# Building the attention mask by slots, queries and keys in one transfer, two weight transfers from ScalarE's queue

## The chip, the cores and the metric

The kernel runs on one core of a Trainium2 chip. Its time is device microseconds (us) of one execution; shown is the median of three runs. One further execution was recorded by the hardware profiler, and every duration below comes from it. PE is TensorE, DVE VectorE, ACT ScalarE, POOL GpSimd, SP SyncE, which issues nearly all transfers.

## The reference

An attention with a band and a few global keys is followed by two feed-forward layers, all in float32:

```
scores = (q @ k^T) / sqrt(64)            # 2 batches, 8 heads, 768 tokens, 64 per head
rel    = query position - key position
keep   = (key < n_global) | (0 <= rel < n_local)          # 8 and 96 at run time
dist   = n_local where only the global rule keeps a key, else |rel|
scores = where(keep, scores - slope[head] * dist, -1e9)
x      = softmax(scores) @ v                              # 1536 tokens x 512
h      = x @ w_in;   x = softplus(h) @ w_out              # 512 -> 2048 -> 512
h      = x @ w_in2;  y = (h * clip(h + 3, 0, 6) / 6) @ w_out2
```

The weights arrive as 64-bit numbers. `n_global` and `n_local` are inputs too, so the mask is computed on the chip.

## The kernel before

**Attention.** The 1536 tokens are 12 blocks of 128 queries. A block needs its own keys, the block before (the band is 96 wide) and the global keys, which are laid over the first 32 columns of the block before. Work goes in quads: `att_s(k)` takes four heads of one block, two quads to a block. A quad has eight score matmuls in the trace for a block with neighbours (`s`, L516; each of the four float32 matmuls runs as two), then four rows on DVE (`pm`, L522: scores plus bias, and the row minimum of the negated sum), four exponentials on ACT (L527), the reciprocal of the sums on DVE (`rs`, L409 and L410), four multiplications by it on POOL (L412), transposes on PE (`ptp`, L550), a copy out of PSUM on ACT (`pT`, L552), and the product with the values on PE (`px`, L568). In the text q0, q1, q2 are the first quads: q0 and q1 belong to block 0, which has no block before and so 128 columns a row; from q2 on a row has 256.

**The mask.** `bias` holds, for each of the 8 heads, three slabs of 128x128: slab 0 for a block's own keys, slab 1 for the block before, slab 2 for a first block (own keys and global keys in one). They are made from `far`, a distance in which forbidden places are huge. L461 to L476 make `far` for all three slabs at once; `counts()` (L780) turns the two integers, which are 64-bit in memory, into floats first. Then ACT multiplies slab 2 by each head's slope (L478, eight operations), and DVE does slabs 0 and 1 in one operation for each head (`bias_of`, L482: four heads ahead of q0, four after it).

**Transfers.** All are issued on SP's queue, in program order: `ns` (the counts), then for each block `qT` and `kT` (queries and keys, laid out by head; block 0 in two pieces each, L442 and L443) and `V` (L447), then the weights (L114). A weight unit is 512 KB.

**Weights.** `unit_convert` (L117 to L146) splits one unit into a high and a low part: absolute value on ACT (L133), clamp on POOL (L136), three integer operations on DVE (L137, L140, L141), a rounding copy on ACT (L145), a subtraction on DVE (L146). The first feed-forward layer needs the high and low parts of the first two units before its first matmul (`hf`, L193).

**Order.** L654 to L661 run the lead: three quads of scores ahead, then for each of five steps some filling matmuls on zeros (`warm`, L651; `FILL`), the transposes, and `LEAD_UNITS` weight units. Before all that stand `WARM` = 12 such matmuls. PE's instructions keep the order in which they are written (`ordered`). The other engines' order comes from a scheduler, except where `keep_in_program_order` fixes it. Each engine works through its own list strictly in turn. After the lead, `Layers.run` weaves the remaining quads into the first layer's matmuls.

**The check.** `check_step` (L615) verifies near the end that the inputs fit the fast way, and sets a flag by which a general way would be taken.

## Time and profile before

| what | value |
|---|---|
| median of 3 runs | 635.11 us (634.53 to 635.13) |
| the profiled execution | 633.73 us |
| its span, first to last instruction | 631.9 us |
| PE busy | 613.0 us, 97% of the span |
| DVE busy | 426.0 us, 67% |
| ACT busy | 381.0 us, 60% |
| POOL busy | 137.3 us, 22% |
| mean granted PE clock | 0.996 |

A busy PE is not PE at its peak: the ends of matmuls are modelled and overlapping ones are merged. The shares are means over stages that differ: while attention and weight conversion run, DVE and ACT are full, and later PE alone is. What a change in the first microseconds is worth is read from that stretch, and from what carries it to the end. 1.8 us of the profiled time lie outside the span.

### The profile page before, as it was taken

What the parts mean: (1) busy time and instruction counts of PE and PEld (TensorE: products, weight loads), DVE (VectorE), ACT (ScalarE), POOL (GpSimd) and SP (SyncE); (2) the same over time, 40 slices, a digit from 0 to 9 for tenths busy, and PEclk for the clock granted to TensorE, in tenths of its full rate; (3) what the DMA queues carried; (4) which work ended last, traced back from release to release, by engine and by line L of the source; (5) the groups of instructions that cost most, each with busy time, mean ns of one, the idle gap of its engine ahead of it and who ended that gap; (6) DMA issues with size and microseconds to landing.
All of it is one profiled execution on the core that took longest, in us unless ns stands there. A gap on an engine that the chain in (4) does not pass through costs nothing.

```text
span 631.9 us, 9656 instructions
## 1 busy us (share of the span) xinstructions
PE 613.0 (97%) x3496; PEld 513.8 (81%) x3496; DVE 426.0 (67%) x893; ACT 381.0 (60%) x808; POOL 137.3 (22%) x180
## 2 busy tenths in 40 slices
PE   8779999999999999999999999999999999999997
PEld 4568987899999888877788888888888888888886
DVE  6988587735799999999998996224943423424252
ACT  6977888774777877777687852425786222222130
POOL 3665454531122233523200410000100000000000
PEclk9989999999999999999999999999999999999999
DMA  8744131011234243333311142001372000001011
GB/s 271 251 170 155 55 101 56 23 26 67 67 106 163 74 158 107 129 103 124 112 62 39 62 134 100 1 1 34 102 248 85 0 1 0 2 0 67 1 67 69
DMA packets 25076, 53.62 MB, mean 85 GB/s; under 512 B 2496, under 2 KB 9152, under 8 KB 25024
## 3 DMA queue, kind: packets, MB, share of 16 engines
q1 hardware_dynamic: 25024, 52.96, 25.4%
q8 instruction: 28, 0.46, 0.3%
q14 instruction: 24, 0.20, 0.1%
HBM read 49.81 MB, written 3.15 MB: 84 GB/s over the span
## 4 chain that ended last, share of the span: by engine, by line
PE 71%; DVE 18%; ACT 6%; issue 2%; DMA 1%; POOL 1%; SPq 0%; POOLq 0%; ACTq 0%; DVEq 0%
PE acc L193 25%; PE h L193 24%; PE accf L193 7%; PE hf L193 6%; ACT pm L527 3%; DVE wa L140 2%; DVE wa L141 2%; PE accz L193 2%; PE hz L193 2%; PE ptp L550 2%; DVE w L146 2%; PE px L568 2%; PE s L516 1%; DVE t L179 1%; DVE t L178 1%
## 5 line engine op out<-in xcount | busy, mean ns | idle before, releaser
L193 PE MATMUL h<-xsh,w 128*128 128x512 f32 x584 | 155.8, 390 | 1.2 <-DVE t L179 1.2
L193 PEld LDWEIGHTS h<-xsh,w 128*128 128x128 f32 x584 | 109.1, 188 | 25.1 <-DVE t L179 2.7
L136 POOL TENSOR_SCALAR wa<-wa 128x512 f32<-128x512 f32 x56 | 69.1, 1239 | 241.3 <-ACT wa L133 241.2
L193 PE MATMUL acc<-w,gh 128*128 128x512 f32 x344 | 106.0, 390 | 0.0
L183 DVE SCALAR_TENSOR_TENSOR t<-t,h 128x512 f32<-128x512 f32 x43 | 29.5, 687 | 77.4 <-ACT t L182 77.3
L185 DVE TENSOR_TENSOR gl<-t,gh 128x512 fp32r<-128x512 f32 x73 | 52.3, 716 | 42.0 <-ACT gh L184 41.8
L193 PE MATMUL h<-xsl,w 128*128 128x512 f32 x292 | 80.6, 390 | 0.0
L182 ACT ACTIVATE t<-h,three 128x512 f32<-128x512 f32 x43 | 29.5, 687 | 83.4 <-PE h L193 83.2
L193 PE MATMUL acc<-gh,w 128*128 128x512 f32 x240 | 77.8, 391 | 0.9 <-ACT gh L184 0.6
L193 PEld LDWEIGHTS acc<-w,gh 128*128 128x128 f32 x344 | 64.6, 188 | 13.3
L184 ACT CAST gh<-t 128x512 fp32r<-128x512 f32 x73 | 45.3, 620 | 43.7 <-PE acc L193 20.4
L412 POOL TENSOR_SCALAR pm<-pm,rs 128x256 f32<-128x256 f32 (+1 forms) x96 | 54.2, 582 | 59.9 <-DVE rs L410 31.8
L193 PE MATMUL acc<-w,gl 128*128 128x512 f32 x172 | 67.1, 390 | 0.0
L193 PEld LDWEIGHTS h<-xsl,w 128*128 128x128 f32 x292 | 54.8, 188 | 11.4
L193 PE MATMUL accf<-ghf,w 128*128 128x256 f32 x288 | 57.3, 288 | 0.0
L193 PEld LDWEIGHTS acc<-gh,w 128*128 128x128 f32 x240 | 44.9, 188 | 11.3 <-ACT gh L184 1.5
L527 ACT ACTIVATE pm<-pm,nm 128x256 f32<-128x256 f32 (+1 forms) x96 | 46.2, 484 | 3.3 <-DVE nm L522 3.1
L193 PE MATMUL hf<-xsh,w 128*128 128x256 f32 x288 | 47.1, 290 | 0.0
L193 PEld LDWEIGHTS accf<-ghf,w 128*128 128x128 f32 x288 | 46.6, 192 | 0.3
L193 PE MATMUL acc<-gl,w 128*128 128x512 f32 x120 | 46.8, 390 | 0.0
L146 DVE TENSOR_TENSOR w<-wa,w 128x512 fp32r<-128x512 f32 x56 | 40.3, 721 | 8.4 <-ACT w L145 8.4
L133 ACT ACTIVATE wa<-raw 128x512 f32<-128x512 f32 x53 | 35.5, 674 | 12.9 <-DVE w L146 7.0
(115 smaller groups left out, 1046.6 us busy)
## 6 DMA issues: line engine op xcount, KB each, us to landing
raw<-in_w2i SPq DMA_DIRECT2D x16, 512.0 KB, 3.3
raw<-in_w2o SPq DMA_DIRECT2D x16, 512.0 KB, 3.2
raw<-in_w1i SPq DMA_DIRECT2D x14, 512.0 KB, 3.4
raw<-in_w1o SPq DMA_DIRECT2D x12, 512.0 KB, 3.3
V<-in_v SPq DMA_DIRECT2D x12, 256.0 KB, 3.5
chk<-in_q SPq DMA_DIRECT2D x12, 256.0 KB, 2.9
chk<-in_k SPq DMA_DIRECT2D x12, 256.0 KB, 2.8
qT<-in_qt SPq DMA_DIRECT2D x11, 256.0 KB, 3.9
```

What stands on the lines that cost most here:

```text
L133: first = nc.scalar.activation(a, raw.bitcast(F32)[:, :, 1], AF.Abs)
L136: nc.gpsimd.tensor_scalar(out=a, in0=a, scalar1=W_HI, scalar2=W_LO, op0=ALU.min, op1=ALU.max)
L140: nc.vector.scalar_tensor_tensor(out=ai, in0=hi, scalar=-2 ** 30, in1=ai, op0=ALU.bitwise_and, op1=ALU.bitwise_or)
L141: nc.vector.scalar_tensor_tensor(out=ai, in0=lo, scalar=29, in1=ai, op0=ALU.logical_shift_right, op1=ALU.bitwise_or)
L146: nc.vector.tensor_tensor(out=wl, in0=a, in1=r32(wh), op=ALU.subtract)
L182: nc.scalar.activation(t1, hf, AF.Relu, bias=self.three[:, 0:1])
L183: nc.vector.scalar_tensor_tensor(out=t3, in0=t1, scalar=6.0, in1=hf, op0=ALU.min, op1=ALU.mult)
L184: nc.scalar.copy(gh, t3)
L185: nc.vector.tensor_tensor(out=gl, in0=t3, in1=r32(gh), op=ALU.subtract)
L193: return self.nc.tensor.matmul(out, lhsT=a, rhs=b, start=start and z == 0, stop=stop and z == len(seq) - 1, **kw)
L412: nc.gpsimd.tensor_scalar(out=t, in0=t, scalar1=rs[:, j:j + 1], scalar2=0.0, op0=ALU.mult, op1=ALU.add)
L527: nc.scalar.activation(pmz, pmz, AF.Exp, bias=nm[:, z:z + 1], scale=-1.0, accum_out=sm[:, z:z + 1])
```

## The change

- The mask is made by slots. `counts()` takes only the low 32-bit word of each integer (`cv`); the full conversion (`full_counts`) moves to `check_step`, which also checks that the low word was enough. `masks(0)` makes `far` for slab 0 and, from it, for slab 2; `masks(1)` makes slab 1 later, ahead of q2's rows.
- Slab 2 of the eight heads is made on three engines: heads 0 and 1 on ACT, 2 to 5 on POOL, 6 and 7 on DVE between q0's second and third row. Slabs 0 and 1 stay on DVE: heads 0 to 3 behind `masks(1)`, heads 4 to 7 behind q2's rows.
- The order on DVE is fixed by hand for this stretch: q0's and q1's reciprocals are held back (`held`) and issued behind q1's rows and behind `masks(1)` with its four slabs.
- Queries and keys of a block stand together in memory and in one buffer (`qk`, three slots); a block is one transfer of 512 KB, block 0 two of 256 KB split by heads.
- The first two weight units are issued on ScalarE's queue, behind its table load.
- The copy of the global keys (`gk`, L500) moves from ACT to POOL. `WARM` goes from 12 to 8.

Line numbers in the pieces of order below are those of the kernel they belong to. On VectorE, from the arrival of the counts to the first rows (`pm`) of q0, the list before reads (`nf`, `cneg`, `cv` are the counts, `gc`, `gfar`, `far`, `rel` the mask's pieces):

```order
L781 CAST cv<-nsb 128x4
L467 COPY rel<-rel 128x128
L782 TENSOR_SCALAR cneg<-cv 128x2
L783 TENSOR_TENSOR cneg<-cneg,cv 128x2
L784 SCALAR_TENSOR_TENSOR nf<-cneg,cv 128x2
L473 TENSOR_SCALAR gfar<-gc,nf 128x384
L474 TENSOR_SCALAR far<-rel,nf 128x384
L475 TENSOR_TENSOR far<-far,rel 128x384
L476 SCALAR_TENSOR_TENSOR far<-gfar,nf,far 128x384
L482 TENSOR_SCALAR bias<-far 128x256 x4
L522 ISA pm_193,nm_194<-s_0_191,bias 128x128
```

and in the change:

```order
L811 CAST cv<-nsb 128x4
L485 TENSOR_SCALAR late<-gc,cv 128x128
L474 TENSOR_SCALAR far<-rel,cv 128x128
L478 TENSOR_TENSOR far<-far,rel 128x128
L481 SCALAR_TENSOR_TENSOR far<-late,cv,far 128x128
L540 ISA pm_171,nm_172<-s_0_169,bias 128x128
L540 ISA nm_172 128x1
L540 ISA pm_171,nm_172<-s_1_170,bias 128x128
```

Between the counts and the first row stand four operations of 128 columns where eight small and wide ones and four slabs stood.

On VectorE between the last row of q1 and the first of q2, before (`rs_212` is q0's reciprocal):

```order
L522 ISA pm_221,nm_222<-s_1_220,bias 128x128
L522 ISA nm_222 128x1
L409 TENSOR_SCALAR rs_212<-sm_195 128x4
L522 ISA pm_250,nm_251<-s_0_248,bias 128x256
```

and in the change (`rs_188` is q0's, `rs_206` q1's):

```order
L411 TENSOR_SCALAR rs_188<-sm_173 128x4
L412 RECIPROCAL rs_188<-rs_188 128x4
L474 TENSOR_SCALAR far<-rel,cv 128x128
L478 TENSOR_TENSOR far<-far,rel 128x128
L481 SCALAR_TENSOR_TENSOR far<-late,cv,far 128x32
L498 TENSOR_SCALAR bias<-far 128x256 x4
L411 TENSOR_SCALAR rs_206<-sm_193 128x4
L540 ISA pm_231,nm_232<-s_0_229,bias 128x256
```

What stood ahead of q0 (slab 1's mask and four double slabs) now stands between q1 and q2, behind a reciprocal that waits for q0's exponentials and ahead of one step that waits for q1's.

On ScalarE from its table load to the copies of q0's transposes, before and then in the change:

```order
L770 ACT_TABLE_LOAD
L500 COPY gk<-kT 128x128
L478 ACTIVATE bias<-far 128x128 x8
L527 ACTIVATE pm_193,sm_195<-pm_193,nm_194 128x128 x4
L527 ACTIVATE pm_221,sm_223<-pm_221,nm_222 128x128 x4
```

```order
L800 ACT_TABLE_LOAD
L116 DMA part_91<-in_w1i 128x1024 x2
L489 ACTIVATE bias<-far 128x128 x2
L549 ACTIVATE pm_171,sm_173<-pm_171,nm_172 128x128 x4
L549 ACTIVATE pm_191,sm_193<-pm_191,nm_192 128x128 x4
```

Six slabs and the copy of the global keys leave ScalarE's list, and two transfers enter it.

The diff, cut:

```diff
-WARM, FILL = 12, (6, 4, 2, 0, 0)
+WARM, FILL = 8, (6, 4, 2, 0, 0)
...
+        self.n_early = 0
...
-        self.nc.sync.dma_start(out=raw.rearrange("p c t -> p (c t)"), in_=self.weights[2 * layer + u][f])
+        queue = self.nc.scalar if x < self.n_early else self.nc.sync
+        queue.dma_start(out=raw.rearrange("p c t -> p (c t)"), in_=self.weights[2 * layer + u][f])
...
-def softmax_rows(nc, sm, rs, pm):
-    nc.vector.tensor_scalar(out=rs, in0=sm, scalar1=EPS, scalar2=None, op0=ALU.add)
+def softmax_rows(nc, sm, rs, pm, keep=lambda i: i):
+    keep(nc.vector.tensor_scalar(out=rs, in0=sm, scalar1=EPS, scalar2=None, op0=ALU.add))
     nc.vector.reciprocal(out=rs, in_=rs)
     for j, t in enumerate(pm):
         nc.gpsimd.tensor_scalar(out=t, in0=t, scalar1=rs[:, j:j + 1], scalar2=0.0, op0=ALU.mult, op1=ALU.add)
...
+        layers.n_early = 2
-        ap2 = actx.enter_context(tc.tile_pool(name="ap2", bufs=3))
...
-        kT = ap1.tile([P, KC, 3, P], F32, name="kT")
+        qk = ap1.tile([P, 3, KC, 2, P], F32, name="qk")
-        qT, V, px = {}, {}, {}
+        V, px = {}, {}
...
         def load_block(n):
-            qT[n] = ap2.tile([P, KC, P], F32, tag="qT", name=f"qT{n}")
-            for cs in (slice(0, 1), slice(1, KC)) if n == 0 else (slice(0, KC),):
-                nc.sync.dma_start(out=qT[n][:, cs], in_=qt[n][:, cs])
-                nc.sync.dma_start(out=kT[:, cs, n % 3, :], in_=kt[n][:, cs])
+            for cs in (slice(0, KC // 2), slice(KC // 2, KC)) if n == 0 else (slice(0, KC),):
+                nc.sync.dma_start(out=qk[:, n % 3, cs], in_=qkt[n][:, cs])
...
         load_block(0)
+        while layers.loaded < layers.n_early:
+            layers.unit_load(layers.loaded)
+            layers.loaded += 1
...
+        rel = tp.tile([P, 2, P], F32, tag="t", name="rel")
+        gc = tp.tile([P, P], F32, tag="t", name="gc")
         far = tp.tile([P, 3, P], F32, tag="t", name="far")
-        gfar = tp.tile([P, 3, P], F32, tag="t", name="gfar")
+        late = tp.tile([P, P], F32, tag="t", name="late")
         bias = ap1.tile([P, H, 3, P], BF16, name="bias")
         iota = dict(allow_small_or_imprecise_dtypes=True)
-        nc.gpsimd.iota(rel[:, 2, :], pattern=[[-1, P]], base=0, channel_multiplier=1, **iota)
-        nc.gpsimd.iota(gc[:, 2, :], pattern=[[1, P]], base=0, channel_multiplier=0, **iota)
+        nc.gpsimd.iota(rel[:, 0, :], pattern=[[-1, P]], base=0, channel_multiplier=1, **iota)
+        nc.gpsimd.iota(gc, pattern=[[1, P]], base=0, channel_multiplier=0, **iota)
         nc.gpsimd.iota(rel[:, 1, :], pattern=[[-1, P]], base=P, channel_multiplier=1, **iota)
-        nc.vector.memset(gc[:, 0:2, :], BIG)
-        nc.vector.tensor_scalar(out=far[:, 2, :], in0=rel[:, 2, :], scalar1=0.0, scalar2=BIG, op0=ALU.is_lt, op1=ALU.mult)
-        nc.vector.tensor_tensor(out=rel[:, 2, :], in0=rel[:, 2, :], in1=far[:, 2, :], op=ALU.add)
-        nc.vector.tensor_copy(rel[:, 0, :], rel[:, 2, :])
+        nc.vector.tensor_scalar(out=late, in0=rel[:, 0, :], scalar1=0.0, scalar2=BIG, op0=ALU.is_lt, op1=ALU.mult)
+        nc.vector.tensor_tensor(out=rel[:, 0, :], in0=rel[:, 0, :], in1=late, op=ALU.add)
         nc.vector.memset(rel[:, 1, 0:MAX_GLOBAL], BIG)
-        nc.vector.tensor_copy(gc[:, 1, 0:MAX_GLOBAL], gc[:, 2, 0:MAX_GLOBAL])
-        counts()
-        ng, nl = nf[:, 0:1], nf[:, 1:2]
-
-        nc.vector.tensor_scalar(out=gfar, in0=gc, scalar1=ng, scalar2=BIG, op0=ALU.is_ge, op1=ALU.mult)
-        nc.vector.tensor_scalar(out=far, in0=rel, scalar1=nl, scalar2=BIG, op0=ALU.is_ge, op1=ALU.mult)
-        nc.vector.tensor_tensor(out=far, in0=far, in1=rel, op=ALU.add)
-        nc.vector.scalar_tensor_tensor(out=far, in0=gfar, scalar=nl, in1=far, op0=ALU.add, op1=ALU.min)
+        ng, nl = counts()
+
+        def masks(z):
+
+            tc.keep_in_program_order(nc.vector.tensor_scalar(
+                out=far[:, z, :], in0=rel[:, z, :], scalar1=nl, scalar2=BIG, op0=ALU.is_ge, op1=ALU.mult
+            ))
+            tc.keep_in_program_order(
+                nc.vector.tensor_tensor(out=far[:, z, :], in0=far[:, z, :], in1=rel[:, z, :], op=ALU.add)
+            )
+            to, n = (far[:, 2, :], P) if z == 0 else (far[:, 1, 0:MAX_GLOBAL], MAX_GLOBAL)
+            tc.keep_in_program_order(nc.vector.scalar_tensor_tensor(
+                out=to, in0=late[:, 0:n], scalar=nl, in1=far[:, z, 0:n], op0=ALU.add, op1=ALU.min
+            ))
+
+        nc.vector.tensor_scalar(out=late, in0=gc, scalar1=ng, scalar2=BIG, op0=ALU.is_ge, op1=ALU.mult)
+        masks(0)
         for h in range(H):
-            nc.scalar.mul(bias[:, h, 2, :], far[:, 2, :], -SLOPES[h] / SCALE)
-
-        def bias_of(hs):
+            if h < 2:
+                nc.scalar.mul(bias[:, h, 2, :], far[:, 2, :], -SLOPES[h] / SCALE)
+            elif h < 6:
+                nc.gpsimd.tensor_scalar(
+                    out=bias[:, h, 2, :], in0=far[:, 2, :], scalar1=-SLOPES[h] / SCALE, scalar2=0.0,
+                    op0=ALU.mult, op1=ALU.add,
+                )
+
+        def bias_of(hs, zs=slice(0, 2)):
             for h in hs:
                 tc.keep_in_program_order(nc.vector.tensor_scalar(
-                    out=bias[:, h, 0:2, :], in0=far[:, 0:2, :], scalar1=-SLOPES[h] / SCALE, scalar2=None, op0=ALU.mult
+                    out=bias[:, h, zs, :], in0=far[:, zs, :], scalar1=-SLOPES[h] / SCALE, scalar2=None, op0=ALU.mult
                 ))
 
-        bias_of(range(H // 2))
-
-        pms, pTs = {}, {}
+        pms, pTs, held = {}, {}, []
         s_tags = [(ps_s, f"s{j}") for j in range(2)]
...
                 if i == 0:
-                    nc.scalar.copy(gk, kT[:, :, slot, 0:MAX_GLOBAL])
+                    nc.gpsimd.tensor_copy(gk, qk[:, slot, :, 1, 0:MAX_GLOBAL])
+            if k == KC // 2:
+                masks(1)
+                bias_of(range(H // 2))
+                softmax_rows(*held.pop(), keep=tc.keep_in_program_order)
...
-                        ps[j][:, a, 0:nsl, :], lhsT=qT[n][hp, 2 * e + a, :], rhs=kT[hp, 2 * e + a, ks, :],
+                        ps[j][:, a, 0:nsl, :], lhsT=qk[hp, slot, 2 * e + a, 0, :], rhs=qk[hp, ks, 2 * e + a, 1, :],
...
-                nc.vector.tensor_tensor_reduce(
+                row = nc.vector.tensor_tensor_reduce(
...
+                if k < KC // 2:
+                    tc.keep_in_program_order(row)
+                if k == 0 and z == 1:
+                    bias_of(range(6, H), slice(2, 3))
                 nc.scalar.activation(pmz, pmz, AF.Exp, bias=nm[:, z:z + 1], scale=-1.0, accum_out=sm[:, z:z + 1])
-            if k == 0:
+            if k == KC // 2:
                 bias_of(range(H // 2, H))
             rs = ap_m.tile([P, 4], F32, tag="rs", name=f"rs{k}")
-            softmax_rows(nc, sm, rs, [pm[:, z, 0:w] for z in range(4)])
+            rows = (nc, sm, rs, [pm[:, z, 0:w] for z in range(4)])
+            if k == 1:
+                softmax_rows(*held.pop(), keep=tc.keep_in_program_order)
+            if k < KC // 2:
+                held.append(rows)
+            else:
+                softmax_rows(*rows)
             if e == KC // 2 - 1 and 1 <= i < NB - 1:
-                nc.scalar.copy(kT[:, :, slot, 0:MAX_GLOBAL], gk)
+                nc.scalar.copy(qk[:, slot, :, 1, 0:MAX_GLOBAL], gk)
...
-            c4 = fp.tile([1, 4], F32, name="c4")
+            c4 = fp.tile([1, 5], F32, name="c4")
+            full_counts()
             nc.vector.tensor_reduce(out=c4[:, 0:1], in_=pf, axis=AX.X, op=ALU.max)
             for z, (src, lim, op) in enumerate((
                 (c4[:, 0:1], SQ_LIMIT, ALU.is_le), (nf[0:1, 0:1], float(MAX_GLOBAL), ALU.is_le),
                 (nf[0:1, 1:2], float(MAX_LOCAL), ALU.is_le), (nf[0:1, 1:2], 1.0, ALU.is_ge),
+                (nf[0:1, 0:1], cv[0:1, 0, 0:1], ALU.is_equal),
...
         def counts():
             tc.keep_in_program_order(nc.vector.tensor_copy(cv, nsb))
-            nc.vector.tensor_scalar(out=cneg, in0=cv[:, :, 0], scalar1=0.0, scalar2=None, op0=ALU.is_lt)
+            return cv[:, 0, 0:1], cv[:, 1, 0:1]
+
+        def full_counts():
+            tc.keep_in_program_order(nc.vector.tensor_scalar(out=cneg, in0=cv[:, :, 0], scalar1=0.0, scalar2=None, op0=ALU.is_lt))
             nc.vector.tensor_tensor(out=cneg, in0=cneg, in1=cv[:, :, 1], op=ALU.add)
             nc.vector.scalar_tensor_tensor(
                 out=nf, in0=cneg, scalar=float(2 ** 32), in1=cv[:, :, 0], op0=ALU.mult, op1=ALU.add
...
-        "qt": blocks(q), "kt": blocks(k),
+        "qkt": np.ascontiguousarray(np.stack([blocks(q), blocks(k)], axis=3)),
```

## Rows read from the trace of the kernel before

**Rows 1.** Busy time by stretch: us, each engine (count), PE clock, DMA share, GB/s.

```profile
20.00:30.00 10.00, 7.09 (x68) 5.08 (x65) 9.97 (x32) 10.00 (x31) 5.84 (x8) 1.00 0.66 202
30.00:40.00 10.00, 7.48 (x74) 6.41 (x74) 10.00 (x30) 7.22 (x20) 7.82 (x12) 1.00 0.63 213
...
43.90:47.20 3.30, 3.30 (x24) 2.32 (x21) 2.23 (x10) 3.27 (x11) 1.76 (x4) 0.50 0.19 57
```

**Rows 2.** Timeline of the head: start, us, engine, line, what [idle before].

```profile
1.29 0.42 SPq L442 DMA_DIRECT2D qT<-in_qt  x1
...
1.31 5.20 PE L651 MATMUL warm<-zeros 128*128 128x512 bf16 x12 [1.31 <-DVE zeros L437]
...
3.46 0.17 DVE L781 CAST cv<-nsb 128x4 f32<-128x4 int32 x1 [1.33 <-DMA nsb<-in_ns]
...
6.29 0.30 ACT L500 COPY gk<-kT 128x128 f32<-128x128 f32 x1 [4.19 <-DMA kT<-in_kt]
...
6.44 1.16 PE L516 MATMUL s<-kT,qT 64*128 64x128 f32 x16
6.49 1.70 ACT L478 ACTIVATE bias<-far 128x128 bf16<-128x128 f32 x8
...
7.30 0.29 DVE L522 CUSTOM_DVE_ANT_0 pm<-s,bias 128x128 f32<-128x128 f32 x1
...
8.10 0.39 ACT L527 ACTIVATE pm<-pm,nm 128x128 f32<-128x128 f32 x1
```

**Rows 3.** Groups by line and form, first 34 us: count, busy us, mean ns.

```profile
L412 POOL TENSOR_SCALAR pm<-pm,rs 128x128 f32<-128x128 f32 x8 | 2.8, 373 | 9.0 <-ACT pm L527 9.0
...
L482 DVE TENSOR_SCALAR bias<-far 128x256 bf16<-128x256 f32 x8 | 1.8, 289 | 0.0
...
L410 DVE RECIPROCAL rs<-rs 128x4 f32<-128x4 f32 x6 | 1.0, 173 | 0.1
...
L466 DVE TENSOR_TENSOR rel<-rel,far 128x128 f32<-128x128 f32 x1 | 0.3, 316 | 0.0
```

**Rows 4.** Block 0's third and fourth piece: queue, size, us from issue to landing.

```profile
qT<-in_qt SPq DMA_DIRECT2D x1, 192.0 KB, 2.5
kT<-in_kt SPq DMA_DIRECT2D x1, 192.0 KB, 3.5
```

**Rows 5.** Timeline from q2's scores to the first weight unit on VectorE.

```profile
8.43 1.23 PE L516 MATMUL s<-kT,qT 64*128 64x256 f32 x8 [0.83 <-DMA kT<-in_kt]
...
9.58 1.47 PE L651 MATMUL warm<-zeros 128*128 128x512 bf16 x6
...
11.18 0.49 ACT L527 ACTIVATE pm<-pm,nm 128x256 f32<-128x256 f32 x1
...
12.68 1.13 PE L516 MATMUL s<-kT,qT 64*128 64x256 f32 x8
...
13.82 1.85 POOL L412 TENSOR_SCALAR pm<-pm,rs 128x256 f32<-128x256 f32 x4
...
15.63 0.62 POOL L136 TENSOR_SCALAR part<-part 128x512 f32<-128x512 f32 x1
...
16.84 0.40 DVE L137 TENSOR_SCALAR part<-part 128x512 int32<-128x512 int32 x1
```

**Rows 6.** Timeline, PE and VectorE, around PE's two long pauses in attention.

```profile
32.02 1.09 PE L568 MATMUL px<-pT,V 128*64 128x128 f32 x16 [3.26 <-ACT kT L533]
...
38.70 0.41 DVE L522 CUSTOM_DVE_ANT_0 pm<-s,bias 128x256 f32<-128x256 f32 x1
...
42.50 0.63 PE L550 MATMUL ptp<-ident,pm 128*128 128x128 f32 x4 [2.38 <-ACT pT L552]
```

**Rows 7.** Timeline where the check's first reduction stands, VectorE and PE's weight loads.

```profile
485.40 0.18 DVE L632 TENSOR_REDUCE m<-sq 128x1 f32<-128x24 f32 x1 [2.12 <-ACT chk L628]
...
485.91 0.69 DVE L185 TENSOR_TENSOR gl<-t,gh 128x512 fp32r<-128x512 f32 x1 [0.33 <-ACT gh L184]
...
486.65 0.19 PEld L193 LDWEIGHTS acc<-w,gl 128*128 128x128 f32 x1 [0.28 <-DVE gl L185]
```

More of the change, by code (lines that the diff above doesn't have):

```diff
@@ L412, in softmax_rows, with fast_path @@
         nc.gpsimd.tensor_scalar(out=t, in0=t, scalar1=rs[:, j:j + 1], scalar2=0.0, op0=ALU.mult, op1=ALU.add)
-def fast_path(tc, ident, three, nf, counts, q, k, qt, kt, v, weights, out, flag):
+def fast_path(tc, ident, three, nf, cv, counts, full_counts, q, k, qkt, v, weights, out, flag):
     with ExitStack() as ctx, ExitStack() as actx:
@@ L764, in general_path, with body @@
         layers.run()
-def body(tc, q, k, v, qt, kt, ns, w1i, w1o, w2i, w2o, out):
+def body(tc, q, k, v, qkt, ns, w1i, w1o, w2i, w2o, out):
     nc = tc.nc
@@ L792, in body @@
         weights = (w1i, w1o, w2i, w2o)
-        fast_path(tc, ident, three, nf, counts, q, k, qt, kt, v, weights, out, flag)
+        fast_path(tc, ident, three, nf, cv, counts, full_counts, q, k, qkt, v, weights, out, flag)
         redo = nc.values_load(flag[0:1, 0:1], min_val=0, max_val=1)
@@ L806, in blocks @@
     def blocks(a):
-        return np.ascontiguousarray(
-            a.reshape(B, KC, 2, NB, P, D).transpose(0, 3, 2, 5, 1, 4)
-        ).reshape(B * NB, P, KC, P)
+        return a.reshape(B, KC, 2, NB, P, D).transpose(0, 3, 2, 5, 1, 4).reshape(B * NB, P, KC, P)
     def words(a, axes=None):
```

2 lines of the change are left out of this document (removed).

## The prediction

> **What bounds the kernel now.** I read the page's table of engines first, then busy time by stretch, then the timeline of the first 17 us. PE is busy for 613.0 of 631.9 us, so time can come only from PE's pauses and its slow stretches. From 20 to 40 us VectorE is full, ScalarE is full for the first half, and PE has about 5.4 us of pauses [rows 1]: the end of this stretch is set by VectorE's list of rows and weight conversions. Behind it PE alone is the bound, and the order of every engine there is the same in both kernels, but for the check near the end. So the change is worth what it moves the full stretch forward, plus what it does to PE's clock in it, less what the check costs.
>
> The reader is to see three things in the timeline of the head. The first row of q0 starts at 7.30, though its scores began at 6.44: VectorE was still at four slabs. The first exponential starts at 8.10, since ScalarE had the copy of the global keys (waiting for block 0's last piece until 6.29) and eight slabs first [rows 2]. And VectorE is full only from 16.84, where the first weight unit reaches it behind POOL's work on q2 (13.82) and the clamp (15.63) [rows 5]. I call that point S.
>
> **The change, step by step** (times in the profiled span; 633.73 us is that execution, 1.38 below the median of 635.11, and differences are carried over to the median unchanged).
>
> *PE's start.* Twelve warm-ups took 5.20 us, 0.433 each; eight take 3.47, so q0's scores can start at 1.31 + 3.47 = 4.78 [rows 2]. Their data, 256 KB issued at 1.29, land 2.5 to 3.5 us later by the two pieces of 192 KB [rows 4], between 3.8 and 4.8: not later than PE. The six warm-ups at 9.58 took 1.47, 0.245 each [rows 5], so the first twelve ran at the lower level (1.2 GHz) and the later ones at 2.4. At the lower level q0's half of the 16 score matmuls takes 1.16 instead of 0.58 [rows 2]; the first row needs three quarters of it, so it starts at 4.78 + 0.87 = 5.7, against 7.30.
>
> *The mask* is no later: the counts at 3.46, 0.17 for the cast, four operations of 128 columns at no more than 0.32 each [rows 3], 0.21 for ScalarE's first slab (eight in 1.70): 5.1. POOL's four slabs are not shown before; its multiplication of the same size takes 0.37 [rows 3], so they end at 4.9 + 1.5 = 6.4, when q1 has not begun its rows. Bounds: 0.21 each (ScalarE's) to 0.46 (four of twice the size took 1.85 [rows 5]); even at 0.46 they end at 6.8, and the last of them is q1's second row's, not needed before.
>
> *ScalarE.* It loses six slabs (6 x 0.21 = 1.3) and the copy (0.3). The first exponential can follow its row by the row's 0.29 and its read-out, 0.4 as an estimate: 6.1. From 8.10 to 11.18 eight exponentials took 3.08 [rows 2, 5], so q0 and q1 end at 9.2. The two issues on its queue fall into its idle time ahead of 6.29; cost nothing.
>
> *VectorE between q1 and q2.* Eight rows and two slabs, at the 0.225 that one of four slabs adds where they overlap (0.29 alone): 5.7 + 2.2 = 7.9. Then q0's two reciprocal steps (0.17 each), slab 1's mask (two operations at 0.32 and one of 32 columns, 0.8 together), four slabs (eight took 1.8 [rows 3]), q1's first step: 7.9 + 0.35 + 0.8 + 0.9 + 0.1 = 10.0, when q1's exponentials are through. So q2's rows start at about 10.0, its exponentials at 10.4 against 11.18. This holds while block 1 lands before 9.1, since three quarters of q2's scores (0.92 of 1.23) must precede; before it landed at 8.43 [rows 5]. I take it to land as before: 192 KB of queries took 2.5 and of keys, which then went into strided pieces, 3.5 [rows 4], and now both go in long lines; but 1 MB of weights runs beside it.
>
> *The point S.* q2's exponentials end 1.96 later (4 x 0.49), at 12.4; reciprocal 0.35, POOL's four 1.85 (now nothing of q1 is in its way), clamp 0.62: S = 15.2 against 16.84, 1.6 earlier. In the change's list q3's two reciprocal steps stand behind S, before they stood ahead of it: 0.35 more to do, leaving 1.3. From S the lists hold the same rows, conversions and subtractions up to q8's rows (38.70), and PE's pause that ends at 42.50 waits for the copy behind q8's exponentials [rows 6]. That PE gets 1.3 us too. Both bounds: VectorE may wait for ScalarE, which is only 0.8 earlier (then 0.5 is left); or it loses nothing and the third unit's earlier place helps (1.7).
>
> *The check.* Three conversions of the counts and one comparison, about 0.17 each, now stand on VectorE between the reduction at 485.40 and `gl`, which began at 485.91 after 0.33 idle, and PE's next weight load waited 0.28 for it [rows 7]. 0.7 of work less 0.33 of cover: 0.3 late, on PE's path. Bounds 0 and 0.4. This part is costed against the change.
>
> *Costed at nothing:* the single transfers of later blocks. PE's two long pauses are put down to copies of ScalarE, not to a transfer [rows 6], so a later landing has that cover; without it a block would wait for its 512 KB, some 2.1 us by block 1 (6.29 to 8.43).
>
> Sum: 1.3 - 0.3 = 1.0 us, 632.7 for a profiled execution, **634.1 us** for the median; with the bounds 633.3 to 634.9.
>
> **The rivals.**
>
> *The slow stretch goes too.* From 43.90 to 47.20 the granted clock was 0.50, the lower level [rows 1]: PE had paused 2.38 us before 42.50. At 2.4 GHz that work takes half, so up to 1.65 us come back. In the change the pause's end moves by 1.3, and what PE does ahead of it by ScalarE's 0.8, so the pause shrinks to some 1.9. For it: a shorter pause. Against: a pause of 3.26 before 32.02 passed without a fall [rows 6], so length alone does not decide. Time: 634.1 - 1.6 = 632.5.
>
> *The weights take turns with block 1.* In the trace every load stands on one queue, and block 1's 512 KB landed 2.1 us behind block 0's (6.29 to 8.43) [rows 2, 5]. If 1 MB on a second queue is served alternately, those 2.1 become up to 4.3, and block 1 lands between 9.5 and 10.6 instead. From 9.1 on each microsecond of it moves q2, S and the end: the 1.0 turns to 0.6 at 9.5 and to a loss of 0.5 at 10.6. Time: 635.1 (634.5 to 635.6); against it speaks the shorter landing of long lines [rows 4]. The Trainium skill bears on this, in "DMA: Bandwidth & Descriptors", section "Queues, rings and completion order": SP and ACT each own one row of rings on the same 16 engines, and an engine goes round the rows that have work. By that rule this is the case, and no run here has shown two queues at once.
>
> *The clock rises late: slower.* Before, it rose behind 5.20 us of unbroken warm-ups, and q1's scores ran at the upper level (16 in 1.16 [rows 2]). Now there are 3.47 us, then scores with possible waits for the second half of block 0, then a pause until block 1 is there. If the clock has not risen when q1's scores end (about 6.7), q2's scores take 2.46 instead of 1.23 and the six warm-ups 2.6 instead of 1.47: q0's transposes start at 8.43 + 5.1 = 13.5 instead of 11.1 [rows 5]. ScalarE's copies of them stand ahead of the first weight unit and of q3's exponentials; they would come at 14.2, against 13.1 before (11.18 + 1.96): 1.1 later, and with the check's 0.3 the end is 1.4 later: 636.5 (635.6 to 637.0). The Trainium skill, "TensorE: Matmul & The Clock Gate", section "What's actually happening", says that the throttled state is the default and that activity releases it; the 0.433 against 0.245 agrees.
>
> **How the numbers follow.** The forecast has 0.37, the slow stretch gone 0.25, weights taking turns 0.18, the late clock 0.20. What a measurement can tell from no change is 0.2%, 1.3 us: faster means under 633.8, slower over 636.4. Of the forecast a good third lies under 633.8 (0.14), the rest within (0.23); the second case is all faster; of the third 0.02 is faster and 0.16 within; of the fourth most counts as slower, since the rows put no upper bound on its price (0.17), and 0.03 lies within. Faster 0.41, same 0.42, slower 0.17. The range 631.9 to 636.4 holds the second case but its lowest end, the first, the third and the lower part of the fourth.
>
> **What would show it.** Right: the first row near 5.7 and the first exponential near 6.1; block 1 landed before 9.1; the first weight unit on VectorE near 15.2; PE resuming near 41.2 in the place of 42.50; `gl` behind the check 0.3 later with PE waiting. A stretch at 0.50 that is shorter or absent shows the first rival; q2's scores after 9.1 with a wait for `qk` the second; six warm-ups near 2.6 us the third. Wrong: the first weight unit not earlier than 16, or a span under 631 or over 635.

## The result: slower, and what the profile after shows

The changed kernel takes 638.1 us (median of 7 runs, 637.1 to 639.9); the kernel before, on the same chip, 635.05 (7 runs, 633.8 to 635.5). The ratio is 1.0058, 95% interval 1.0047 to 1.0069: 3 us slower by the medians, 3.7 by the ratio, where 1.0 us faster was forecast and 636.4 was the upper end of the range. The profiled execution spans 636.2 us against 631.9.

The timeline of the head of the changed kernel, on the columns of [rows 2] (names as there; `qk` holds queries and keys, L681 are the warm-ups, L534 scores, L540 rows, L549 exponentials, L489 ScalarE's slabs, L139 the first weight unit on VectorE):

```profile
0.84 0.89 ACTq L116 DMA_DIRECT2D part<-in_w1i  x2
...
1.28 1.68 SPq L443 DMA_DIRECT2D qk<-in_qkt  x3
...
1.31 3.60 PE L681 MATMUL warm<-zeros 128*128 128x512 bf16 x8 [1.31 <-DVE zeros L439]
...
5.64 0.17 DVE L811 CAST cv<-nsb 128x4 f32<-128x4 int32 x1 [3.72 <-DMA nsb<-in_ns]
...
7.08 0.51 ACT L489 ACTIVATE bias<-far 128x128 bf16<-128x128 f32 x2 [4.99 <-DVE far L481]
...
7.92 2.21 PE L534 MATMUL s<-qk 64*128 64x128 f32 x16 [3.02 <-DMA qk<-in_qkt]
...
9.30 0.29 DVE L540 CUSTOM_DVE_ANT_0 pm<-s,bias 128x128 f32<-128x128 f32 x1 [2.25 <-PE s L534]
...
9.64 0.40 ACT L549 ACTIVATE pm<-pm,nm 128x128 f32<-128x128 f32 x1 [2.05 <-DVE nm L540]
...
10.40 2.30 PE L534 MATMUL s<-qk 64*128 64x256 f32 x8 [0.27 <-DVE nm L540]
...
12.62 2.74 PE L681 MATMUL warm<-zeros 128*128 128x512 bf16 x6
...
14.11 0.51 ACT L549 ACTIVATE pm<-pm,nm 128x256 f32<-128x256 f32 x1 [1.29 <-DVE nm L540]
...
19.37 0.43 DVE L139 TENSOR_SCALAR part<-part 128x512 int32<-128x512 int32 x1 [0.58 <-POOL part L138]
...
45.80 0.63 PE L578 MATMUL ptp<-ident,pm 128*128 128x128 f32 x4 [2.58 <-ACT pT L580]
```

Read it from the top. ScalarE's queue asks for 1 MB of weights at 0.84, before SyncE asks for the queries and keys at 1.28. The counts, 2 KB that SyncE asked for at 0.84 as before, are converted at 5.64 instead of 3.46 [rows 2]. The scores of q0 wait 3.02 us for their data and start at 7.92 instead of 6.44, at half the speed (2.21 for the 16 that took 1.16). The first row is 2.0 us late, the first exponential 1.5, q2's exponentials 2.9, point S 2.5 (16.84 [rows 5]), PE's restart 3.3 (42.50 [rows 6]). So 3.3 of the 4.3 us between the two spans are lost by PE's restart. Of the rest, some 0.8 is lost between 203.3 and 303.3 us, where PE is busy for 97.56 us (98.31 in the same stretch before, 3.3 us earlier); no run says why.

The packets of the DMA queues between 2.0 and 4.5 us, of the kernel before (queue, count, MB, share of the 16 engines):

```profile
q1 hardware_dynamic: 614, 0.36, 67.6%
```

and of the changed kernel, where q1 is SyncE's and q10 ScalarE's (a packet of the profile is one line of one partition, such as 16 bytes of the counts or 4 KB of weights):

```profile
q10 hardware_dynamic: 71, 0.29, 49.3%
q1 hardware_dynamic: 120, 0.00, 2.2%
```

SyncE's queue, which moved 0.36 MB in this stretch before, is still at the counts' 16-byte packets, 128 of them, eight to an engine; block 0 stands behind them. Yet no more bytes moved than before (0.29 MB), and the engines were half idle. It is not bandwidth that ran out. By the start of the last of the counts' 128 packets, at 5.12, ScalarE's queue had started 119 of its own.

The loss reaches the rows through block 0: ScalarE's slabs began at 7.08, but the first row waited for the scores until 9.30, and these for `qk` until 7.92.

The stretches that answer to [rows 1], of the changed kernel:

```profile
20.00:30.00 10.00, 7.67 (x68) 5.17 (x66) 9.97 (x32) 9.68 (x30) 6.04 (x9) 1.00 0.46 145
30.00:40.00 10.00, 7.94 (x72) 6.23 (x70) 10.00 (x34) 9.55 (x28) 8.38 (x12) 1.00 0.67 215
46.90:50.20 3.30, 3.30 (x24) 2.27 (x20) 1.73 (x9) 3.27 (x10) 2.06 (x4) 0.50 0.19 41
```

VectorE is full as before, and the stretch at 0.50 has only moved along, from 43.90 to 46.90. The end of the check, for [rows 7], and the stretch around it in the kernel before and in the changed one:

```profile
490.17 0.67 DVE L187 TENSOR_TENSOR gl<-t,gh 128x512 fp32r<-128x512 f32 x1
...
490.89 0.19 PEld L195 LDWEIGHTS acc<-w,gl 128*128 128x128 f32 x1 [0.35 <-DVE gl L187]
```

```profile
455.00:492.00 37.00, 37.00 (x164) 30.44 (x163) 14.01 (x23) 26.46 (x66) 0.61 (x1) 1.00 0.48 150
...
455.00:492.00 37.00, 37.00 (x164) 30.40 (x163) 17.51 (x34) 27.65 (x70) 1.05 (x2) 1.00 0.57 169
```

A weight load waits 0.35 there, 0.28 before. PE's matmuls have no pause in either: they are busy for 37.00 of 37.00 us.

### The profile page after: what moved, and what is told of

Read it like the earlier page. It is cut to its first block, busy times and chain, and to the rows that moved or that the text cites. A ratio compares the mean times of both kernels' runs of the same rounds, so it can differ in the third digit from the quotient of the medians.

```text
span 636.2 us, 9630 instructions
## 1 busy us (share of the span) xinstructions
PE 615.3 (97%) x3492; PEld 515.5 (81%) x3492; DVE 426.3 (67%) x896; ACT 380.1 (60%) x800; POOL 140.3 (22%) x186
## 4 chain that ended last, share of the span: by engine, by line
PE 71%; DVE 19%; ACT 5%; issue 2%; POOL 1%; DMA 1%; SPq 0%; POOLq 0%; ACTq 0%; DVEq 0%
PE acc L195 24%; PE h L195 24%; PE accf L195 6%; PE hf L195 6%; DVE wa L142 3%; DVE wa L143 2%; PE accz L195 2%; PE hz L195 2%; DVE w L148 2%; PE s L534 2%; ACT pm L549 2%; PE ptp L578 2%; PE px L596 2%; DVE t L181 1%; DVE t L180 1%
## 5 line engine op out<-in xcount | busy, mean ns | idle before, releaser
L187 DVE TENSOR_TENSOR gl<-t,gh 128x512 fp32r<-128x512 f32 x73 | 51.9, 711 | 41.2 <-ACT gh L186 41.1
L195 PEld LDWEIGHTS acc<-w,gh 128*128 128x128 f32 x344 | 64.6, 188 | 13.4
L414 POOL TENSOR_SCALAR pm<-pm,rs 128x256 f32<-128x256 f32 (+1 forms) x96 | 55.9, 599 | 50.8 <-DVE rs L412 33.2
L549 ACT ACTIVATE pm<-pm,nm 128x256 f32<-128x256 f32 (+1 forms) x96 | 46.3, 485 | 7.4 <-DVE nm L540 6.0
L540 DVE CUSTOM_DVE_ANT_0 pm<-s,bias 128x256 f32<-128x256 f32 (+1 forms) x96 | 33.1, 395 | 16.5 <-PE s L534 16.4
```

The costliest lines, as they stand in the source:

```text
L187: nc.vector.tensor_tensor(out=gl, in0=t3, in1=r32(gh), op=ALU.subtract)
L195: return self.nc.tensor.matmul(out, lhsT=a, rhs=b, start=start and z == 0, stop=stop and z == len(seq) - 1, **kw)
L414: nc.gpsimd.tensor_scalar(out=t, in0=t, scalar1=rs[:, j:j + 1], scalar2=0.0, op0=ALU.mult, op1=ALU.add)
L540: row = nc.vector.tensor_tensor_reduce(out=pmz, in0=ps[z % 2][:, z // 2, 0:nsl, :].rearrange("p s t -> p (s t)"), in1=bias[:, 4 * e + z, m ...
L549: nc.scalar.activation(pmz, pmz, AF.Exp, bias=nm[:, z:z + 1], scale=-1.0, accum_out=sm[:, z:z + 1])
```

## The experiments

Theory A: what costs is that the weights on ScalarE's queue go out ahead of the counts and of block 0. Theory B: the new mask code costs. Theory C: eight warm-ups leave the clock low. More came up on the way. All times are medians over five rounds, with the kernel before on the same chip beside them. The ratios are to it; they are estimated together with their intervals and are not the quotients of the two medians.

### One part undone, one part alone

*The weights back on SyncE's queue.*

```
-        layers.n_early = 2
+        layers.n_early = 0
```

> The changed kernel with the first two units of weights asked for on SyncE's queue again, behind block 1 (everything else of the change stays). Theory A (the two 512 KB loads on ScalarE's queue, issued at 0.84 us, delayed the counts from 3.46 to 5.64 and block 0 past the end of the warm-ups): counts converted near 3.5, first score row near 5.7 to 6.0, first exponential near 6.2, first unit's last step on VectorE near 15 to 15.5 in place of 19.37, time 633 to 635. Theory B (the new mask code, the held softmax rows and the slabs on GpSimd cost the time, wherever the weights come from): first row early, but the first unit's last step still past 18, time 637 to 638.5. Theory C (eight warm-ups are too few for the clock, whatever the loads do): counts and first row early, but the matmuls behind them still at the lower clock until past 14, first unit's last step 16.5 to 18, time 635.5 to 637.

635.96 against 634.37, ratio 1.0021 (1.0005 to 1.0037). Its head:

```profile
3.66 0.17 DVE L811 CAST cv<-nsb 128x4 f32<-128x4 int32 x1 [1.73 <-DMA nsb<-in_ns]
...
5.43 0.29 DVE L540 CUSTOM_DVE_ANT_0 pm<-s,bias 128x128 f32<-128x128 f32 x1 [0.38 <-ACT bias L489]
...
5.77 0.40 ACT L549 ACTIVATE pm<-pm,nm 128x128 f32<-128x128 f32 x1 [0.17 <-DVE nm L540]
...
8.78 2.17 PE L534 MATMUL s<-qk 64*128 64x256 f32 x8 [2.80 <-DVE far L481]
...
10.86 0.42 DVE L540 CUSTOM_DVE_ANT_0 pm<-s,bias 128x256 f32<-128x256 f32 x1 [0.94 <-PE s L534]
```

Counts, first row (5.7 forecast) and first exponential (6.1) come as Theory A says, so B falls for the head. But q2's scores ran at the lower clock (2.17 for 1.23), behind a pause of 2.8, and q2's rows came at 10.86. The clock had risen at 4.0, while the warm-ups ran, and was at 0.50 again from 7.4 to 14.3. Point S is at 16.91 (the 19.37 that the expectation calls the first unit's last step is S too, its first step on VectorE), and S and the time lie in Theory C's ranges. No gain is left of the early start.

*Twelve warm-ups in the changed kernel.*

```
-WARM, FILL = 8, (6, 4, 2, 0, 0)
+WARM, FILL = 12, (6, 4, 2, 0, 0)
```

> The changed kernel with twelve warm-up matmuls in place of eight; the weights stay on ScalarE's queue. The warm-ups then end near 6.6 us, and the scores of the first quad still wait for their data until 7.9. Theory A in its first form (late data alone): nothing before 7.9 changes, the first unit's last step stays near 19.4, time 638. Theory C (the low clock after the idle 3.0 us is what costs): the gap is 1.3 us in place of 3.0, the clock is up by the second quad's scores, the six warm-ups take 1.5 in place of 2.6 us, the first unit's last step comes near 17.0 to 17.8, time 635.5 to 636.5.

639.61, ratio 1.0071 (1.0047 to 1.0096): no better. In its profile the counts came later still, at 6.31, PE waited 2.58 for `qk`, and q0's scores took 2.19 again. The clock had risen at 5.2, while the twelve warm-ups ran, and was back at 0.50 through the scores and the six warm-ups (columns of [rows 1]):

```profile
8.70:15.40 6.70, 6.44 (x30) 4.10 (x31) 5.35 (x35) 3.18 (x16) 2.33 (x6) 0.50 1.03 416
```

So more warm-ups do not help while the data are late, but what the low clock costs this run does not test.

*Both: weights on SyncE's queue, twelve warm-ups.* Both edits above.

> The changed kernel with the weights on SyncE's queue and twelve warm-ups: of the change only the masks, the held rows, the slabs on three engines and the merged loads of queries and keys stay. Theory A and C alike: counts at 3.5, clock up near 6.3, first row near 6.9 to 7.1 (the warm-ups end at 6.5), first unit's last step 15.5 to 16.3, time 633.5 to 635. Theory B: first unit's last step past 17, time 636 or more. Against the run with eight warm-ups it prices the warm-ups once the data are early.

635.04 against 634.37, ratio 1.0008 (0.9997 to 1.0019). First row 6.52, first exponential 6.85, 1.25 before the kernel before. Point S is at 15.25, where the forecast had it, yet no time is won; see the mask below. B, which wanted 636 or more, falls.

*The kernel before with only the early loads.* The edit is the change's own: `queue = self.nc.scalar if x < self.n_early else self.nc.sync`, and the loop over `layers.unit_load` behind `load_block(0)`.

> The kernel before with one edit: the first two units of weights are asked for on ScalarE's queue. Theory A: issued at 0.84, before the queries and keys; counts land near 5.6 in place of 3.46, the first score row comes 1.5 to 2.2 us late (9 to 9.5 in place of 7.30), the first unit's last step at 18.5 to 19, time 636.5 to 637.5. Theory B: within 0.5 us of the kernel before, time 635. Theory C: the twelve warm-ups bring the clock up at 6.3 as before, so that only the data's delay shows: time 635.5 to 636.5.

638.03, ratio 1.0060 (1.0043 to 1.0078): this one edit gives the whole loss. Counts at 6.42, first row at 10.44, with twelve warm-ups and the old mask; counts and row are later than A said (5.6; 9 to 9.5). The clock was at 0.50 from 10.3 to 17.1 in this profile, so a part of the loss can be the clock's; the run with one unit below takes that out.

### When, how much, and in what pieces

*The same loads on ScalarE's queue, issued behind its two slabs.*

```
+            if x < self.n_early:
+                self.tc.keep_in_program_order(load)
...
-        while layers.loaded < layers.n_early: ...      (behind load_block(0))
+        while layers.loaded < layers.n_early: ...      (behind the slabs of the first mask)
```

> The changed kernel with one edit: ScalarE issues the two loads of weights behind its two mask slabs (near 5.6 us) in place of at 0.84; they stay on its own queue, and eight warm-ups stay. Theory A (what costs is that the loads are ahead of the counts and of block 0): counts near 3.6, first row near 5.4, first exponential near 5.8, as with the weights on SyncE's queue; time 635 to 636.3. Theory D (a second queue costs by itself, whenever it is used, since it takes turns with block 1 and the values): block 1 lands later than 8.8, with the second quad's scores past 9.5, time 636.5 to 638.

634.65 against 634.39, ratio 1.0003 (0.9991 to 1.0015). Issued at 5.09, the loads cost nothing that can be told, with eight warm-ups; q2's scores start at 8.41, not past 9.5. But the two queues hardly met: between 5.10 and 8.60 the only queue that moved anything is SyncE's.

```profile
q1 hardware_dynamic: 440, 1.20, 92.8%
```

The first packet of weights started at 8.64, 3.5 us behind its issue (1.3 us in the changed kernel), when block 1 was there; why so late, no run shows. The clock was up from 6.8 on, so eight warm-ups do not by themselves leave it low, as Theory C has it. So the early issue is what costs, and whether a second queue beside block 1 costs by itself (Theory D) this run does not test.

*Half of the dose, in the kernel before:* `n_early = 1`.

> The kernel before with only the first unit of weights (512 KB) asked for on ScalarE's queue at 0.84, the second on SyncE's as before: half of the dose that cost 3.7 us. Theory A: counts land near 4.9 (3.46 without, 6.42 with two), block 0's last piece near 8, time 635.8 to 636.8, about half of the loss. A theory in which the second queue costs by its use alone, not by its bytes: the full loss, 638.

637.43, ratio 1.0056 (1.0043 to 1.0069): a miss. Half of the bytes cost 3.0 of 3.7 us. Counts at 5.65, and the clock was not in it, as the stretch behind the warm-ups and the six warm-ups show (L488 are VectorE's slabs, L533 the exponentials):

```profile
5.65 0.17 DVE L787 CAST cv<-nsb 128x4 f32<-128x4 int32 x1 [3.52 <-DMA nsb<-in_ns]
...
8.48 0.90 DVE L488 TENSOR_SCALAR bias<-far 128x256 bf16<-128x256 f32 x4
...
10.28 0.40 ACT L533 ACTIVATE pm<-pm,nm 128x128 f32<-128x128 f32 x1
...
11.40 1.47 PE L657 MATMUL warm<-zeros 128*128 128x512 bf16 x6
...
5.20:46.00 40.80, 29.71 (x244) 20.79 (x244) 35.02 (x134) 33.84 (x114) 24.26 (x41) 1.00 0.71 247
```

In this kernel the loss runs through the counts, at least up to the first exponential: VectorE's slabs are 2.2 us late (they began at 6.29 before, behind the mask), the first exponential too (8.10 [rows 2]), as the counts are. So neither bytes nor clock set the price. Theory G: the engines take turns between the two queues, and each of the counts' eight packets on an engine waits for one 4 KB packet. Such a packet took 0.28 us on average in the changed kernel between 2.0 and 4.5 (49.3% of 16 engines for 2.5 us, over 71 packets) and 0.21 here (49.2%, over 95), and one unit has eight on an engine, as many as the counts. Eight turns cost 1.7 to 2.2 us as an estimate; measured 2.2 (5.65 less 3.46). The second unit adds bytes, but few turns: here too 119 packets of weights had started by the counts' last, at 5.11. Theory H: the bytes ahead.

*The counts first on ScalarE's queue*, ahead of the weights:

```
-        nc.sync.dma_start(out=nsb.rearrange(...), in_=ns.partition_broadcast(P))
+        nc.scalar.dma_start(out=nsb.rearrange(...), in_=ns.partition_broadcast(P))
```

> The changed kernel with one edit: the 2 KB of counts are asked for on ScalarE's queue, ahead of the two units on the same queue; queries and keys stay on SyncE's. Theory G (the 16 DMA engines take one packet of each queue in turn: the counts' 128 packets of 16 bytes, eight to an engine, each stood behind a 4 KB packet of 0.2 us, and block 0 behind them on its queue; with one unit that is the same eight turns, which is why half of the dose cost nearly all): counts near 3.6 again; block 0's first half, eight packets of 2 KB to an engine at 0.1, takes eight turns of 0.3 in place of 0.1, so its scores start near 6.0 (4.46 with the weights on SyncE's queue, 7.92 in the changed kernel); time 636 to 637. Theory H (1 MB asked for first simply takes the bandwidth, whatever the packets): counts no earlier than 5, scores at 7.5 to 8, time 637.5 to 638.5.

636.65 against 634.5, ratio 1.0026 (1.0014 to 1.0039). Its head:

```profile
4.23 0.17 DVE L811 CAST cv<-nsb 128x4 f32<-128x4 int32 x1 [2.31 <-DMA nsb<-in_ns]
4.83 1.23 PE L534 MATMUL s<-qk 64*128 64x128 f32 x8
...
6.84 1.22 PE L534 MATMUL s<-qk 64*128 64x128 f32 x8 [0.78 <-DMA qk<-in_qkt]
```

The same bytes, and a third (by the medians) to a half (by the ratios) of the loss is gone. It is not quite as expected: the counts now take turns with block 0's 2 KB packets (0.6 late), and block 0's first half meets only the small counts and is there by 4.83, its second half meets the weights (6.84). Block 1 meets them too (q2's scores at 9.42, behind a wait of 1.36 for `qk`), and the clock rose only at 13.4, so this run does not price the counts alone.

*The weights in 1 KB pieces,* four loads for each unit:

```
+        for z in range(pieces):
+            cs = slice(z * step, (z + 1) * step)
+            queue.dma_start(out=raw.rearrange(...)[:, cs], in_=self.weights[2 * layer + u][f][:, cs])
```

> The changed kernel with one edit: each of the two early units is asked for in four loads of 128 KB, 1 KB to a partition, on ScalarE's queue from 0.84 on (eight issues in place of two). Theory G (turns, packet by packet): a 1 KB packet takes some 0.05 to 0.06 us by 0.032 for 512 bytes and 0.1 for 2 KB, so eight turns of the counts' packets cost 0.4 to 0.5 in place of some 1.6 to 2.0: counts near 4.0 to 4.3 (3.66 without early weights, 5.64 with 4 KB packets), block 0's first half near 5 to 5.5, time 635 to 636.5. Theory H (the bytes ahead): by the time the counts are asked for the same queue holds 128 to 256 KB and gets more at 128 KB each 0.43 us, counts past 5, scores past 7, time 637 to 638.5.

638.26, ratio 1.0068 (1.0051 to 1.0084). The landings are G's, the time is not:

```profile
0.84 7.80 ACTq L120 DMA_DIRECT2D part<-in_w1i  x8
...
3.55 0.17 DVE L815 CAST cv<-nsb 128x4 f32<-128x4 int32 x1 [1.63 <-DMA nsb<-in_ns]
...
8.69 0.51 ACT L493 ACTIVATE bias<-far 128x128 bf16<-128x128 f32 x2 [6.60 <-DMA part<-in_w1i]
```

The counts come at 3.55, as without any early weights. But the eight issues held ScalarE until 8.64, the last four of them for 4.92, and its slabs waited behind them. So the same edit with one unit, four issues, in the kernel before:

> The kernel before with the first unit of weights on ScalarE's queue from 0.84 on, as in the run that cost 3.0 us (1.0056), but in four loads of 128 KB with 1 KB to a partition. The four issues end near 2.7, ahead of ScalarE's first work at 6.3. Theory G (turns): counts near 3.7 to 4.2 in place of 5.65, block 0's last piece near 7 in place of 7.9, first row 7.4 to 8, time 634.4 to 635.8 (ratio 1.000 to 1.002). Theory H (512 KB ahead cost their bytes): counts 5.6, time 637 as with 4 KB packets.

635.64 against 634.44, ratio 1.0014 (1.0006 to 1.0023); in 4 KB pieces it was 1.0056.

```profile
0.84 1.86 ACTq L120 DMA_DIRECT2D part<-in_w1i  x4
...
3.62 0.17 DVE L791 CAST cv<-nsb 128x4 f32<-128x4 int32 x1 [1.48 <-DMA nsb<-in_ns]
...
8.27 0.40 ACT L537 ACTIVATE pm<-pm,nm 128x128 f32<-128x128 f32 x1
```

```profile
q10 hardware_dynamic: 430, 0.39, 46.2%
q1 hardware_dynamic: 459, 0.20, 37.5%
```

(the queues again between 2.0 and 4.5). More weights moved beside SyncE's loads than in the changed kernel, 0.39 MB against 0.29, and SyncE's queue went one for one with them, packet for packet. The counts' last packet started at 3.19, behind 117 packets of weights, as many as in the 4 KB case. By the ratios three quarters, by the medians three fifths of the loss hung on the packets' size. This is G, and H falls. The four issues also ask for the unit piece by piece, over 1.86 us; but with 430 packets moved ScalarE's queue did not run dry, so that is not what spared the counts. The last 1.2 us stand where block 0 and block 1 come late (q0's last scores at 7.29, q2's at 9.26 with a wait of 1.03 for `kT`).

### Where the expected gain went

*The whole mask ahead of the first rows*, with weights on SyncE's queue and twelve warm-ups: `masks(1)` and `bias_of(range(H // 2))` move from `if k == KC // 2` in `att_s` to behind the first mask's slabs.

> The changed kernel with the weights on SyncE's queue, twelve warm-ups, and the other two slots' mask and their first four slabs (1.95 us on VectorE) ahead of the first quad's rows, where VectorE idles, in place of between the second and the third quad's rows. Theory E (with the weights out of the way the gain at ScalarE's start is lost where it waits 1.5 us for the third quad's rows, which come behind that mask at 10.87): rows of the first quad near 6.9, of the third near 9.7 to 9.9, ScalarE without a pause until 12, its exponentials from 10.3 (11.18 before), time 0.5 to 1.0 less than with the mask in the middle (635.0), so 634.0 to 634.5. Theory F (block 1's landing at 8.7 and the lists behind decide, the mask's place does not): third quad's rows still past 10.3, time 635.0 as with the mask in the middle.

633.93 against 634.39, ratio 0.9996 (0.9985 to 1.0006). With the mask in the middle, VectorE and ScalarE had this between q1's rows and q2's (L580 is the copy of q0's transposes):

```profile
8.83 0.26 DVE L474 TENSOR_SCALAR far<-rel,cv 128x128 f32<-128x128 f32 x1
...
9.73 1.05 DVE L498 TENSOR_SCALAR bias<-far 128x256 bf16<-128x256 f32 x4
...
10.87 0.41 DVE L540 CUSTOM_DVE_ANT_0 pm<-s,bias 128x256 f32<-128x256 f32 x1
...
11.56 0.37 ACT L580 COPY pT<-ptp 128x256 f32<-128x256 f32 x1 [1.53 <-PE ptp L578]
...
11.83 0.51 ACT L549 ACTIVATE pm<-pm,nm 128x256 f32<-128x256 f32 x1
```

and with the mask early, q2's rows and exponentials and PE's restart are:

```profile
10.13 0.42 DVE L540 CUSTOM_DVE_ANT_0 pm<-s,bias 128x256 f32<-128x256 f32 x1 [0.41 <-PE s L534]
...
10.75 0.49 ACT L549 ACTIVATE pm<-pm,nm 128x256 f32<-128x256 f32 x1
...
41.58 0.63 PE L578 MATMUL ptp<-ident,pm 128*128 128x128 f32 x4 [1.86 <-ACT pT L580]
```

ScalarE goes from q1's exponentials to q2's without a pause, 0.43 ahead of the kernel before, and PE restarts 0.9 earlier (41.58 for 42.50 [rows 6]). The order of the two medians (633.93, 635.04) is Theory E's, that the mask's place used up the gain. But the two intervals overlap, and the copy's place changed as well: with the mask in the middle it stands ahead of q2's exponentials and waits for PE's transposes, with the mask early it stands behind them. So E is supported, not shown.

*The same with the late loads on ScalarE's queue* (both edits together):

> The kernel with twelve warm-ups and the whole mask ahead of the first rows, with the two units on ScalarE's queue, issued behind its two slabs (5.1): the parts of the change that cost nothing, together. Theory A and E: the head as with the weights on SyncE's queue (rows at 7.3, third quad's rows near 10, exponentials 10.7), time 633.6 to 634.2. Rival (a second queue costs by its use): later scores of block 1, past 9.5, time 635 or more.

634.04 against 634.5, ratio 0.9985 (0.9971 to 0.9999). Of all kernels here it is the only one whose interval lies below the kernel before, by a hair, by less than the 0.2% that one comparison can tell (0.5 us by the medians), and as one of fourteen comparisons.

*Matmuls in PE's pauses*, against the stretch at the lower clock: `PRE = (0, 0, 0, 4, 10)` and `warm_up(PRE[p])` ahead of `att_step("v", ...)`, in the kernel with the early mask and in the kernel before.

> The kernel with the weights on SyncE's queue, twelve warm-ups and the whole mask ahead of the first rows, and with fourteen more warm-up matmuls in TensorE's pauses: four ahead of the fourth quad's values (pause of 1.25 us) and ten ahead of the fifth's (2.21 us). Theory K (the stretch at the lower clock behind such a pause costs up to 1.7 us and comes from the pause): no stretch at 0.50 between 25 and 45, time 0.5 to 1.2 below the kernel without them (633.93), so 632.8 to 633.4. Rival (the pauses are too short or the stretch follows an earlier one): the stretch stays or moves behind the pause at 40, the fills cost 0 to 0.5: 633.9 to 634.5.

> The kernel before with the same fourteen matmuls in TensorE's pauses at 24.3 and 28.8 (1.25 and 3.26 us). Theory K: no stretch at 0.50 behind 25 to 45, time 0.5 to 1.2 less than the kernel before. Rival: the stretch stays, at 43.8 behind the pause of 2.38, and the time is the same as before.

1.0017 (1.0001 to 1.0033) and 0.9998 (0.9984 to 1.0012). The fills fell a quad earlier than meant, four near 20 and ten from 24 on, and the long pause behind them stayed (3.22 us before 33.20 in the one, 2.19 before 32.04 in the other). Both profiles have a stretch at half speed from 33 or 34 on. So Theory K is not tested for that pause; filling the earlier ones gained nothing.

*The kernel before once more*, for a second profile:

> The kernel before once more, for a second profile: which of its stretches repeat. Head as before (counts 3.4 to 3.7, first row 7.3, block 1's scores 8.4 to 8.6, clock up near 6.3). If the late losses of the other profiles (0.4 to 0.8 us near 270 to 300 and 0.6 to 2 us near 470 to 490) come from how the check's loads happen to land, this profile shows some of them too; if they belong to the changed head, it shows none.

634.46, span 632.7. Its head repeats (counts 3.59, q0's first row 7.24, q2's scores 8.32). Its stretches do not:

```profile
25.60:28.80 3.20, 3.20 (x23) 2.87 (x24) 3.20 (x14) 3.20 (x10) 2.07 (x5) 0.50 0.54 181
32.40:35.60 3.20, 3.20 (x23) 2.87 (x20) 3.20 (x10) 2.54 (x9) 1.02 (x2) 0.50 0.89 309
43.90:47.20 3.30, 3.30 (x38) 2.80 (x35) 2.75 (x10) 3.27 (x11) 1.71 (x4) 1.00 0.35 110
```

The same program had its clock at 0.50 elsewhere and twice, and not from 43.90 on. PE's matmuls lost another 0.5 us between 455 and 492, waiting for `gl` (none in the first profile, nor in the changed kernel's), as in most other kernels' profiles. Such losses belong to no part of the change.

## Why the prediction was wrong

**The failed step** is the third, on ScalarE: "The two issues on its queue fall into its idle time ahead of 6.29; cost nothing." The issues did fall into idle time, but the loads that they start took turns with the counts and block 0 on the DMA engines. A term put at nothing measured some 3.5 us: the changed kernel takes 638.1, and 634.65 with the same loads issued 4.3 us later; alone in the kernel before they cost 3.7 (638.03 against 634.37). I priced the issuing engine's time and took the landings of the counts and of block 0 from a trace with a single queue: "the mask is no later: the counts at 3.46", "between 3.8 and 4.8". Both fell with it (5.64; 7.92).

**The second rival** had the mechanism and the wrong victim. It let the two queues take turns and counted bytes, so it went to block 1, a load of 512 KB, with at most 0.5 us of loss. Turns are counted in packets, and the load with the most turns for its size is the smallest: 2 KB in 128 packets. Its sign, a wait for `qk` ahead of q2's scores, is not in the changed kernel (10.40, behind a row's `nm`); the wait of 3.02 stands ahead of q0's. It is there where the counts were spared (1.36 and 1.03). The Trainium skill's rule named there ("DMA: Bandwidth & Descriptors", section "Queues, rings and completion order"), that an engine goes round the rows that have work, agrees with the runs: 119 packets of weights beside the counts' 128, and 459 packets beside 430. The run with the late loads does not show it: ScalarE's queue, asked at 5.09, moved nothing until 8.64.

**The third rival** showed its sign, 2.74 for six warm-ups where 2.6 was said; the clock rose only at 16.2 (6.3 before). It is a companion, not the cause: with the clock up the loss is there (3.0 us with one unit), and with late loads eight warm-ups cost nothing that can be told (1.0003). They are not safe either: with the weights on SyncE's queue eight took 1.0021 and twelve 1.0008, whose intervals overlap. What the clock adds inside the changed kernel no run separates.

**The steps that held, once the loads were out of the way:** PE's start (4.46, 4.78 said), the mask (5.09 for ScalarE's slab, 5.1 said), first row 5.43 (5.7) and first exponential 5.77 (6.1). The row is early by luck: the clock rose at 4.0 in that profile, and the forecast had it low. S at 15.25 (15.2), with twelve warm-ups, is luck too: the first unit's conversion stands ahead of three of q2's exponentials there, where the forecast had it behind them. With eight warm-ups, as forecast, S came at 16.91 and 16.27.

**The step from S to PE's restart failed too.** In the kernel with S at 15.25 S is 1.6 early, but PE's pause before 32.02 [rows 6] ends at 32.59, 0.6 late. (Its restart at 43.78 instead of 41.2 proves less: the clock was at 0.50 from 32.0 to 38.8 there.) With the mask early S is at 17.82, 1.0 late, and PE restarts 0.9 early. S was no mark of progress. The gain at the first exponential was used up behind q1's exponentials: q2's rows stood behind VectorE's mask (10.87 for 10.0), and ScalarE paused for 1.53, by the trace for PE's transposes, whose copy came ahead of q2's exponentials. Which of the two decides is not separated. So without the early loads the rest of the change gives no gain that can be told (1.0003 to 1.0021), not 1.0 us.

**The check** was read from the wrong row. The 0.28 and the 0.33 are waits of a weight load and of VectorE, and the prediction put 0.3 "on PE's path"; PE's matmuls have no pause there in either profile, so the term measured nothing that can be told. The weight load's own wait grew by 0.07, while it varies from 0.28 to 0.66 between two profiles of the kernel before.

**The first rival** did not come: the pause ahead of PE's restart is 2.58 (2.38 before, 1.9 forecast), and the stretch at 0.50 is as long as before, from 46.90 on.

## What to carry over

Before a load goes to a second queue, look at what is in flight on the first one then, and count its packets: a tiny load spread over 128 partitions can pay one packet of the other queue for each of its own. Ask for bulk after the small loads on which the start depends have landed, even on an idle engine's queue. And a gain is followed to the engine that never pauses: an instruction that merely comes earlier in a reordered list proves none.
